# Attention's reciprocals of the sums, from columns to rows: by TensorE and 512-byte rows in place of 4-byte elements

## The chip, the core and the metric

One core of a Trainium2 chip runs the whole program: TensorE (PE, with its weight loads as PEld), VectorE (DVE), ScalarE (ACT), GpSimd (POOL), and SyncE (SP), which issues nearly all transfers from one queue. The metric is the time of one launch on the device in microseconds. Shown are the median of the runs and one profiled execution with its trace.

## The reference

Attention over 32 heads with pooled queries, then two feed-forward stages, which the change leaves alone. The attention, cut to what is computed:

```
q_pool = q.reshape(B, H, S // 2, 2, D).mean(axis=3)          # B 4, H 8, S 1152, D 64
scores = 1 / sqrt(D) * matmul(q_pool, k.transpose(0, 1, 3, 2))
attn = exp(scores - max(scores))
attn = attn / (sum(attn, axis=-1) + 1e-9)
out = matmul(attn, v)
```

## The kernel before

The 32 heads are worked off as 16 pairs (p), each pair in 9 tiles (t) of 128 queries, 144 tiles (g) in all. A tile's 1152 keys stand as 1024 columns, `ps_s` (L82, L85), and a rest of 128 columns, `ps_r` (L95, L98), on 128 partitions; the rest uses 128 of the 512 columns of its PSUM bank, of which there is one. VectorE takes the maximum (L105 over `ps_s`, L106 over `ps_r`), ScalarE the exponentials (L117, L119), whose accumulators give the sums as a column, one number for each query's partition. TensorE transposes the exponentials (L131), VectorE and ScalarE copy them back (L149, L147) into `aw_et`, and TensorE multiplies them by v (L190, "av" below). The result has the queries along its columns, so the reciprocal of the sums is wanted as a row, repeated on 64 partitions for each of the two heads: `aw_rb`.

The way from column to row goes through DRAM, twice in a pair: chunk c = 0 after the fourth tile (t = 3), and c = 1 after the ninth (t = 8). `sums` adds and inverts (L158, L159) and issues the column writes into `rdram`, one element of 4 bytes for each query (two transfers at L164, and for c = 1 two more at L167). `spread` issues the loads that repeat a row of 1024 bytes on 64 partitions (L175, and L177 for the fifth tile, 256 bytes). `out` multiplies av's result by it (L198, L200), which frees the one PSUM bank of av, and issues the store of the pair (L201). av for a chunk is cut into four pieces, one for each of four tiles; the multiply comes in the tile after the last piece.

The order is written out as events with due times (`at`): what is to happen for a tile g stands at g plus a fraction, all events are sorted, and every engine gets its instructions in that order. `sums` is due at g + 2.13, `spread` at g + 5.05, the pieces of av at .5 of each tile, the multiply at 1.11 of the next. The loads of the next pair's q and k (L53, L55; `load_qk`) are due in its first two tiles, v (L60) in the seventh. In between run steps that prepare weights of the next stage: a load `bg_raw` (L295), VectorE steps on `bg_e` (L311 to L330), stores `wi_d` (L338, L339). SyncE issues in program order and waits in its queue for what each transfer needs.

At the end of attention SyncE issues the load of `m_a_wsh` (L387) between the last column writes and the last loads of rows, and the next stage's first matmul (L501) waits until PSUM is free, which is after the last multiply.

Of the kernel before, what the change touches and what calls it, by code (L numbers as in the profile page):

```python
# [5 lines left out]
F32 = mybir.dt.float32  # L6
# [23 lines left out]
def attention(tc, nc, ap, cst, xT, bg, hooks):  # L30
# [5 lines left out]
    with ExitStack() as ctx:  # L36
        wrk = Pool(ctx.enter_context(tc.tile_pool(name="a_wrk", bufs=2, side="right")), "aw")
        early = ctx.enter_context(ExitStack())
        opr = Pool(early.enter_context(tc.tile_pool(name="a_op", bufs=2)), "ao")
        ps = Pool(ctx.enter_context(tc.tile_pool(name="a_ps", bufs=1, space=PSUM)), "ps")  # L40
        ident = cst["ident"]

        KIND = [(0, 0), (1, 0), (0, 1), (1, 1), (0, 2), (1, 2), (0, 3), (1, 3), None]
        NT = NP * NTL
        P = {}
        E, ET, SUM, MX, TP = {}, {}, {}, {}, {}
        rdram = tc.dram_tile([NP, 2, 6, 128], F32, name="rdram")

        def load_qk(p, h):
# [51 lines left out]
        def maximum(g):  # L101

            d = E[g]
            m = d["m"] = wrk([128, 2], F32, "mx", bufs=4)
            nc.vector.tensor_reduce(out=m[:, 0:1], in_=d["s"], op=ALU.min, axis=AX.XY)  # L105
            nc.vector.tensor_scalar(out=wrk([128, 128], F32, "junk", bufs=1), in0=d["r"][:, 0:128], scalar1=m[:, 0:1], scalar2=None,  # L106
                                    op0=ALU.min, op1=ALU.min, accum_out=m[:, 1:2])

# [44 lines left out]
        def sums(p, c):  # L153

            n = 4 if c == 0 else 5
            s = SUM.pop((p, c))
            rs = wrk([128, 6], F32, f"rs{c}")
            nc.vector.scalar_tensor_tensor(out=rs[:, 0:n], in0=s[:, 0:n, 0], scalar=1e-9, in1=s[:, 0:n, 1], op0=ALU.add, op1=ALU.add)  # L158
            nc.vector.reciprocal(out=rs[:, 0:n], in_=rs[:, 0:n])  # L159
            d = rdram[p, c]  # L160
            with nc.allow_non_contiguous_dma(reason="a pair's sums, from columns to rows"):

                for h in range(2):
                    nc.sync.dma_start(d[3 * h:3 * h + 2].rearrange("c q -> q c"), rs[:, h:4:2])  # L164
                if c:
                    for h in range(2):
                        nc.sync.dma_start(d[3 * h + 2:3 * h + 3].rearrange("c q -> q c"), rs[:, 4:5])  # L167
            P[p]["rb", c] = wrk([128, 320], F32, f"rb{c}", bufs=1)

        def spread(p, c):  # L170
            rb, d = P[p]["rb", c], rdram[p, c]
            for h in range(2):
                o = slice(64 * h, 64 * h + 64)
                row = d[3 * h:3 * h + 3].rearrange("c q -> (c q)").unsqueeze(0)
                nc.sync.dma_start(rb[o, 0:256], row[:, 0:256].to_broadcast([64, 256]))  # L175
                if c:
                    nc.sync.dma_start(rb[o, 256:320], row[:, 256 + 64 * h:320 + 64 * h].to_broadcast([64, 64]))  # L177

        AVQ = []

# [40 lines left out]
        def at(time, f, *a):  # L221
            events.append((time, len(events), f, a))
# [6 lines left out]
        for g in range(NT):  # L229
            p, t = divmod(g, NTL)  # L230
            at(g, scores, g)
            at(g + .2, scores_rest, g)
            at(g + .6, maximum, g)
            at(g + 1.15, exps, g)
            at(g + 1.98, transp, g, 0)
            at(g + 2.1, back, g, 0, "v")
            at(g + 2.15, transp, g, 1)
            at(g + 2.4, back, g, 1, "a")
            if t == 3:
                at(g + 2.13, sums, p, 0)  # L240
                at(g + 5.05, spread, p, 0)
                at(g + 3.45, push, p, 0)
            if t == 8:
                at(g + 2.13, sums, p, 1)
                at(g + 5.05, spread, p, 1)
                at(g + 3.45, push, p, 1)
            if p + 1 < NP:
                if t in (0, 1):
                    at(g + .3 if p else g + 1.3, load_qk, p + 1, t)
                if t in (3, 4):  # L250
                    at(g + .3, prep, p + 1, t - 3, nc.gpsimd)
                if t == 6:
                    at(g + .3, load_v, p + 1)
            if t % 9 not in (3, 4, 5) and g > 3:
                at(g + .12, step, "v")
                at(g + .42, step, "a")
# [922 lines left out]
def fused(tc, q, k, v, w_in, w_sp, b_sp, w_out, w_g, w1, w2, consts, out):  # L1179
# [7 lines left out]
    with ExitStack() as ctx, tc.manual_schedule():  # L1187
# [6 lines left out]
        hooks = {"raw": lambda: m1.begin_v(keep([128, 4096], F32R, "wv").rearrange("p (n k c) -> p n k c", n=2, k=4)),  # L1194
                 "S": m1.begin, "x1": m1.begin_x1, "T": lambda: m1.split_x(0, m1.x0), "end": m1.begin_u}
        attention(tc, nc, ap, cst, xT, bg, hooks)
        bgp.close()
        tab = Pool(ctx.enter_context(tc.tile_pool(name="tab", bufs=1, side="right")), "tab")
# [77 lines left out]
```

## Time and profile before

| | us |
|---|---|
| runs of the kernel before | 1138.47, 1144.91 (median), 1147.83 |
| the profiled execution | 1142.15 |
| its span, first to last instruction | 1140.4 |
| TensorE busy in the span | 1017.6 |
| VectorE busy | 743.2 |

Sizes by the page's list of transfers: the two halves of a pair's q have 576 KB each, of its k 320 KB each, so a half of q and k together 896 KB (917 thousand bytes); the first load, of the identity, 64 KB; `m_a_wsh` 1024 and 128 KB. 30,858 of the program's 68,128 packets are under 512 bytes.

How to read it: the busy share is an average over stages with different limits. Attention takes the first 592 us of the span, and a page or an answer for all of it mixes tiles in which the engines follow each other without a gap with tiles in which all of them wait. What ended a wait is what counts. In the rows, "[4.70 <-DMA aw_rb<-rdram]" means that the engine sat idle for 4.70 us and that this transfer's landing ended it; SPq is SyncE's queue; a transfer's piece in the chain of waits runs from its issue to its landing.

### The profile page before, as it was taken

The numbers are of one execution on the slowest core, as the hardware profiler recorded it, in microseconds if no ns is written. First come the engines' busy times: TensorE is split into PE (matmuls) and PEld (weight loads), VectorE is DVE, ScalarE is ACT, GpSimd is POOL, SyncE is SP. The second block draws the span as 40 slices with busy tenths as digits, with TensorE's granted clock in tenths as the row PEclk, the third lists the DMA queues.
The fourth block names the chain that finished last, engine by engine and source line by source line (L and its number), as shares of the span: only waits on it lengthen the run. The fifth ranks groups of instructions, "written<-read, shape, count | busy, mean of one in ns | idle before, by whom it ended". The sixth has DMA issues, their size and how long they took to land.

```text
span 1140.4 us, 19804 instructions
## 1 busy us (share of the span) xinstructions
PE 1017.6 (89%) x7500; PEld 685.5 (60%) x7500; DVE 743.2 (65%) x1329; ACT 595.6 (52%) x1172; POOL 229.1 (20%) x189
## 2 busy tenths in 40 slices
PE   6679878799989969989947999999999999999997
PEld 3234434344444434444436898899777777777775
DVE  5558766577876757766718861423378877888784
ACT  4346645466656646655614332212237767776773
POOL 1001110111110111110025341122121413133221
PEclk9789988999999989989978899999999999999999
DMA  5346745456756756737153211200283314111750
GB/s 153 85 84 103 113 90 124 70 114 113 109 117 126 88 95 121 94 105 144 36 151 111 66 53 39 75 1 1 91 285 143 120 47 176 37 38 50 279 222 26
DMA packets 68128, 116.78 MB, mean 102 GB/s; under 512 B 30858, under 2 KB 39218, under 8 KB 66488
## 3 DMA queue, kind: packets, MB, share of 16 engines
q1 hardware_dynamic: 64304, 104.38, 39.4%
q0 software_dynamic: 3680, 11.02, 2.9%
q8 instruction: 63, 1.03, 0.5%
q14 instruction: 41, 0.34, 0.2%
q10 hardware_dynamic: 40, 0.01, 0.0%
HBM read 165.61 MB, written 19.48 MB: 162 GB/s over the span
## 4 chain that ended last, share of the span: by engine, by line
PE 44%; issue 20%; DMA 19%; DVE 10%; POOL 3%; ACT 2%; SPq 2%; another core or an unknown queue 0%; POOLq 0%; DVEq 0%; ACTq 0%
PE ps_av L190 10%; PE ps_t L131 8%; DMA aw_rb<-rdram 7%; DMA rdram<-aw_rs 6%; PE ps_s L82 5%; DMA er_x<-x,tab_gi 4%; PE m_ps_v L608 4%; PE m_ps_u L556 4%; PE m_ps_u L542 3%; PE m_ps_v L501 3%; POOL er_x L983 2%; PE ps_r L95 2%; DVE aw_et L149 2%; DVE aw_mx L105 2%; PE ps_s L85 1%
## 5 line engine op out<-in xcount | busy, mean ns | idle before, releaser
L131 PEld LDWEIGHTS ps_t<-keep_ident,aw_e 64*128 64x128 f32 x2592 | 107.6, 143 | 225.8 <-DVE aw_et L149 145.0
L190 PE MATMUL ps_av<-aw_et,aw_v 128*64 128x320 f32 (+1 forms) x1152 | 175.3, 433 | 38.2 <-DVE aw_xo L200 38.2
L105 DVE TENSOR_REDUCE aw_mx<-ps_s 128x1 f32<-128x1024 f32 x144 | 174.8, 1214 | 15.4 <-PE ps_s L82 8.4
L131 PE MATMUL ps_t<-keep_ident,aw_e 64*128 64x64 f32 x2592 | 146.3, 239 | 42.8 <-DVE aw_et L149 32.7
L149 DVE COPY aw_et<-ps_t 128x640 f32<-128x640 f32 x144 | 118.7, 824 | 95.4 <-PE ps_t L131 84.3
L119 ACT ACTIVATE aw_e<-ps_s,aw_mx 128x1024 f32<-128x1024 f32 x144 | 159.2, 1105 | 0.0
L82 PE MATMUL ps_s<-ao_k,ao_q 64*128 64x512 f32 x512 | 148.2, 659 | 7.3 <-DMA ao_k<-in_k 5.9
L117 ACT ACTIVATE aw_e<-ps_r,aw_mx 128x128 f32<-128x128 f32 x144 | 52.9, 368 | 163.8 <-DVE aw_junk L106 163.2
L190 PEld LDWEIGHTS ps_av<-aw_et,aw_v 128*64 128x64 f32 x1152 | 74.3, 142 | 89.8 <-DVE aw_xo L200 39.5
L147 ACT ACTIVATE aw_et<-ps_t 128x512 f32<-128x512 f32 x144 | 86.0, 597 | 77.2 <-PE ps_t L131 70.5
L354 DVE TENSOR_TENSOR eb_w2l<-er_r,eb_w2h 128x1024 fp32r<-128x1024 f32 x88 | 103.5, 1218 | 4.6 <-ACT eb_w2h L350 4.4
L354 DVE TENSOR_TENSOR eb_w1l<-er_r,eb_w1h 128x1024 fp32r<-128x1024 f32 x66 | 78.8, 1221 | 34.1 <-ACT eb_w1h L350 34.1
L350 ACT ACTIVATE eb_w2h<-er_r 128x1024 fp32r<-128x1024 f32 x88 | 88.7, 1068 | 0.6 <-PE ep_yp L1056 0.3
L71 POOL TENSOR_TENSOR ao_qr<-ao_qr 128x576 f32<-128x576 f32 x30 | 42.4, 1414 | 213.5 <-DMA ao_qr<-in_q 181.2
L350 ACT ACTIVATE eb_w1h<-er_r 128x1024 fp32r<-128x1024 f32 x66 | 67.8, 1072 | 18.1 <-DMA er_r<-in_w 8.5
L1056 PE MATMUL ep_yp<-eb_w2h,ew_hth 128*128 128x512 f32 x176 | 71.1, 404 | 0.3 <-ACT ew_hth L350 0.3
L1056 PE MATMUL ep_yp<-eb_w2h,ew_htl 128*128 128x512 f32 x176 | 70.2, 399 | 0.2 <-DVE ew_htl L354 0.2
L1056 PE MATMUL ep_yp<-eb_w2l,ew_hth 128*128 128x512 f32 x176 | 69.1, 393 | 0.0
L1062 POOL DMA_INDIRECT out<-ew_y,tab_si x22 | 22.4, 1017 | 202.6 <-DVE ew_y L1061 176.7
L106 DVE TENSOR_SCALAR_CACHE_REDUCE aw_junk<-ps_r,aw_mx 128x128 f32<-128x128 f32 x144 | 50.6, 351 | 19.1 <-PE ps_r L95 0.6
L501 PE MATMUL m_ps_v<-keep_wv,m_a_xh 128*128 128x512 f32 x144 | 47.0, 400 | 14.7 <-issue 13.7
L354 POOL TENSOR_TENSOR bg_l<-bg_e,bg_h 128x256 fp32r<-128x256 f32 x16 | 11.6, 727 | 237.7 <-ACT bg_h L350 237.7
(234 smaller groups left out, 1905.0 us busy)
## 6 DMA issues: line engine op xcount, KB each, us to landing
er_r<-in_w SPq DMA_DIRECT2D x45, 2048.0 KB
ao_qr<-in_q SPq DMA_DIRECT2D x32, 576.0 KB
ao_k<-in_k SPq DMA_DIRECT2D x32, 320.0 KB
aw_v<-in_v SPq DMA_DIRECT2D x16, 576.0 KB
xT<-aw_xo SPq DMA_DIRECT2D x16, 288.0 KB
bg_raw<-in_w_in SPq DMA_DIRECT2D x16, 256.0 KB
aw_rb<-rdram SPq DMA_DIRECT2D x64, 64.0 KB
er_r<-in_w SPq DMA_DIRECT2D x16, 256.0 KB
```

Of the source, the lines that this page charges most:

```text
L82: nc.tensor.matmul(d["s"][:, i, :], r["q", h][rows, 128 * n:128 * n + 128], r["k", h][rows, 0:512], start=True, stop=True)
L105: nc.vector.tensor_reduce(out=m[:, 0:1], in_=d["s"], op=ALU.min, axis=AX.XY)
L117: nc.scalar.activation(out=e[:, 8, :], in_=d["r"][:, 0:128], func=AF.Exp, bias=d["m"][:, 1:2], scale=-1.0, accum_out=s[:, col, 1:2])
L119: nc.scalar.activation(out=e[:, 0:8, :].rearrange("p k c -> p (k c)"), in_=d["s"].rearrange("p i c -> p (i c)"), func=AF.Exp, bias=d["m"][ ...
L131: nc.tensor.transpose(t[:, i, 64 * (k - k0):64 * (k - k0) + 64], E[g]["e"][o, k, :], ident[o, o])
L147: nc.scalar.activation(out=o, in_=i, func=AF.Copy)
L149: nc.vector.tensor_copy(o, i)
L190: nc.tensor.matmul(box["t"][64 * h:64 * h + 64, 0:n], v[:, h, k, :], et[:, k, h, 0:n], start=k == 0, stop=k == 8)
L350: nc.scalar.activation(out=hi, in_=src, func=AF.Copy)
L354: (nc.gpsimd if eng_lo == "p" else nc.vector).tensor_tensor(out=lo, in0=src, in1=hi.bitcast(F32), op=ALU.subtract)
L501: nc.tensor.matmul(pv, xx[xi][:, k, tile(i, j)], wv[:, wj, k, :], start=n == 0, stop=n == 11)
L1056: nc.tensor.matmul(pt, hT[hi][:, c, 128 * o:128 * o + 128], W2[wi][:, f, :], start=f == 0 and (hi, wi) == (0, 0), stop=f == 7 and (hi, wi) ...
```

## The change

The reciprocals stay as they are (L158 and L159 before, L164 and L165 now), but no transfer starts there. `sums_turn`, due at g + 2.25, has TensorE transpose the 4 or 5 columns of reciprocals into as many rows, in columns 128 to 255 of the bank that holds the rest of the scores of tile g + 2 (L171). `maximum` for that tile copies the rows to SBUF (L109), between its two instructions, and SyncE writes them to DRAM as rows of 512 bytes (L110). The last chunk of all has no tile behind it, and does the same in a bank of its own (`sums_last`). `spread` is due one tile earlier, at g + 4.05, and its loads read two rows of 512 bytes where they read one of 1024, since the rows of DRAM now stand in the order of the tiles.

```diff
--- before.py
+++ after.py
@@ -43,7 +43,7 @@
         KIND = [(0, 0), (1, 0), (0, 1), (1, 1), (0, 2), (1, 2), (0, 3), (1, 3), None]
         NT = NP * NTL
         P = {}
-        E, ET, SUM, MX, TP = {}, {}, {}, {}, {}
+        E, ET, SUM, RS, TP = {}, {}, {}, {}, {}
         rdram = tc.dram_tile([NP, 2, 6, 128], F32, name="rdram")
 
         def load_qk(p, h):
@@ -103,6 +103,12 @@
             d = E[g]
             m = d["m"] = wrk([128, 2], F32, "mx", bufs=4)
             nc.vector.tensor_reduce(out=m[:, 0:1], in_=d["s"], op=ALU.min, axis=AX.XY)
+            if "row" in d:
+                q, c, n = d["row"]
+                row = wrk([6, 128], F32, f"row{c}")
+                nc.vector.tensor_copy(row[0:n], d["r"][0:n, 128:256])
+                nc.sync.dma_start(rdram[q, c, 0:n], row[0:n])
+                P[q]["rb", c] = wrk([128, 320], F32, f"rb{c}", bufs=1)
             nc.vector.tensor_scalar(out=wrk([128, 128], F32, "junk", bufs=1), in0=d["r"][:, 0:128], scalar1=m[:, 0:1], scalar2=None,
                                     op0=ALU.min, op1=ALU.min, accum_out=m[:, 1:2])
 
@@ -157,24 +163,31 @@
             rs = wrk([128, 6], F32, f"rs{c}")
             nc.vector.scalar_tensor_tensor(out=rs[:, 0:n], in0=s[:, 0:n, 0], scalar=1e-9, in1=s[:, 0:n, 1], op0=ALU.add, op1=ALU.add)
             nc.vector.reciprocal(out=rs[:, 0:n], in_=rs[:, 0:n])
-            d = rdram[p, c]
-            with nc.allow_non_contiguous_dma(reason="a pair's sums, from columns to rows"):
-
-                for h in range(2):
-                    nc.sync.dma_start(d[3 * h:3 * h + 2].rearrange("c q -> q c"), rs[:, h:4:2])
-                if c:
-                    for h in range(2):
-                        nc.sync.dma_start(d[3 * h + 2:3 * h + 3].rearrange("c q -> q c"), rs[:, 4:5])
+            RS[p, c] = rs
+
+        def sums_turn(p, c, g):
+
+            n = 4 if c == 0 else 5
+            nc.tensor.transpose(E[g]["r"][0:n, 128:256], RS.pop((p, c))[:, 0:n], ident)
+            E[g]["row"] = (p, c, n)
+
+        def sums_last(p, c):
+
+            t = ps([128, 512], F32, "r")
+            nc.tensor.transpose(t[0:5, 0:128], RS.pop((p, c))[:, 0:5], ident)
+            row = wrk([6, 128], F32, f"row{c}")
+            nc.vector.tensor_copy(row[0:5], t[0:5, 0:128])
+            nc.sync.dma_start(rdram[p, c, 0:5], row[0:5])
             P[p]["rb", c] = wrk([128, 320], F32, f"rb{c}", bufs=1)
 
         def spread(p, c):
+
             rb, d = P[p]["rb", c], rdram[p, c]
             for h in range(2):
                 o = slice(64 * h, 64 * h + 64)
-                row = d[3 * h:3 * h + 3].rearrange("c q -> (c q)").unsqueeze(0)
-                nc.sync.dma_start(rb[o, 0:256], row[:, 0:256].to_broadcast([64, 256]))
+                nc.sync.dma_start(rb[o, 0:256].rearrange("p (c q) -> p c q", c=2), d[h:4:2].unsqueeze(0).to_broadcast([64, 2, 128]))
                 if c:
-                    nc.sync.dma_start(rb[o, 256:320], row[:, 256 + 64 * h:320 + 64 * h].to_broadcast([64, 64]))
+                    nc.sync.dma_start(rb[o, 256:320], d[4:5, 64 * h:64 * h + 64].to_broadcast([64, 64]))
 
         AVQ = []
 
@@ -238,11 +251,16 @@
             at(g + 2.4, back, g, 1, "a")
             if t == 3:
                 at(g + 2.13, sums, p, 0)
-                at(g + 5.05, spread, p, 0)
+                at(g + 2.25, sums_turn, p, 0, g + 2)
+                at(g + 4.05, spread, p, 0)
                 at(g + 3.45, push, p, 0)
             if t == 8:
                 at(g + 2.13, sums, p, 1)
-                at(g + 5.05, spread, p, 1)
+                if g + 2 < NT:
+                    at(g + 2.25, sums_turn, p, 1, g + 2)
+                else:
+                    at(g + 2.25, sums_last, p, 1)
+                at(g + 4.05, spread, p, 1)
                 at(g + 3.45, push, p, 1)
             if p + 1 < NP:
                 if t in (0, 1):
```

Where it moves instructions. TensorE, after the fourth tile of the second pair; `ps_s` and `ps_r` are the scores and their rest, `ps_t` transposes, `ps_av` av, `aw_rs` the reciprocals. Before:

```order
L82 MATMUL ps_s_655<-ao_k_10_156,ao_q_12_229 128x512 x2
L131 MATMUL ps_t_665<-keep_ident_65,aw_e_627 128x64 x8
L95 MATMUL ps_r_678<-ao_k_10_156,ao_q_12_229 128x128
L190 MATMUL ps_av_549<-aw_et_292,aw_v_88 64x320 x6
L131 MATMUL ps_t_691<-keep_ident_65,aw_e_675 128x64 x10
```

Now:

```order
L82 MATMUL ps_s_657<-ao_k_10_156,ao_q_12_229 128x512 x2
L137 MATMUL ps_t_664<-keep_ident_65,aw_e_629 128x64 x8
L95 MATMUL ps_r_677<-ao_k_10_156,ao_q_12_229 128x128
L171 MATMUL ps_r_677<-keep_ident_65,aw_rs_57_661 4x128
L203 MATMUL ps_av_551<-aw_et_294,aw_v_88 64x320 x6
```

One transpose into the same bank as the rest has come in, between the rest and av. After a ninth tile it stands between the rest and the next ten transposes instead.

VectorE, after the ninth tile of the first pair (`aw_mx` the maximum, `aw_row` the new rows). Before:

```order
L158 SCALAR_TENSOR_TENSOR aw_rs_39_476<-aw_sum_20_267 128x5
L159 RECIPROCAL aw_rs_39_476<-aw_rs_39_476 128x5
L105 TENSOR_REDUCE aw_mx_510<-ps_s_467 128x1
L106 TENSOR_SCALAR aw_junk_512,aw_mx_510<-ps_r_497,aw_mx_510 128x128
L149 COPY aw_et_528<-ps_t_514 128x5x128
```

Now:

```order
L164 SCALAR_TENSOR_TENSOR aw_rs_40_478<-aw_sum_19_264 128x5
L165 RECIPROCAL aw_rs_40_478<-aw_rs_40_478 128x5
L105 TENSOR_REDUCE aw_mx_508<-ps_s_469 128x1
L109 COPY aw_row_44_510<-ps_r_494 5x128
L112 TENSOR_SCALAR aw_junk_514,aw_mx_508<-ps_r_494,aw_mx_508 128x128
L155 COPY aw_et_530<-ps_t_516 128x5x128
```

The copy of the rows has come in between the two instructions of the maximum.

SyncE's queue at the same place, from the second half of the next pair's q and k to the load of the rows. Before:

```order
L164 DMA rdram<-aw_rs_39_476 128x2x1 x2
L167 DMA rdram<-aw_rs_39_476 128x1 x2
L53 DMA ao_qr_15_499<-in_q 128x1152
L55 DMA ao_k_16_501<-in_k 128x640
L338 DMA wi_d<-bg_h_504 128x256
L339 DMA wi_d<-bg_l_505 128x256
L175 DMA aw_rb_40_483<-rdram 64x256
L177 DMA aw_rb_40_483<-rdram 64x64
```

Now:

```order
L53 DMA ao_qr_15_497<-in_q 128x1152
L55 DMA ao_k_16_499<-in_k 128x640
L356 DMA wi_d<-bg_h_502 128x256
L357 DMA wi_d<-bg_l_503 128x256
L110 DMA rdram<-aw_row_44_510 5x128
L188 DMA aw_rb_45_513<-rdram 64x2x128
L190 DMA aw_rb_45_513<-rdram 64x64
```

Four column writes ahead of q and k have gone, and one write of five rows has come in behind them.

## Rows read from the trace of the kernel before

**Rows 1.** The page, part 4: the chain that ended last, by line.
```profile
PE ps_av L190 10%; PE ps_t L131 8%; DMA aw_rb<-rdram 7%; DMA rdram<-aw_rs 6%; PE ps_s L82 5%; DMA er_x<-x,tab_gi 4%; PE m_ps_v L608 4%; PE m_ps_u L556 4%; PE m_ps_u L542 3%; PE m_ps_v L501 3%; POOL er_x L983 2%; PE ps_r L95 2%; DVE aw_et L149 2%; DVE aw_mx L105 2%; PE ps_s L85 1%
```

**Rows 2.** Waits of 0 to 590 us: waiter <- releaser: total us, times, longest.
```profile
PE ps_av L190 <- DVE aw_xo L200: 38.2, 7, 8.2
...
DVE bg_e L311 <- DMA bg_raw<-in_w_in: 10.7, 1, 10.7
```

**Rows 3.** The chain of waits, 165 to 200 us: start, us, what.
```profile
165.31 0.38 SPq L164
...
166.25 8.49 DMA rdram<-aw_rs
...
175.31 10.80 DMA aw_rb<-rdram
...
186.81 1.98 PE ps_av L190 x8
...
189.51 1.81 PE ps_s L82 x4
...
195.87 1.01 PE ps_av L190 x8
...
197.34 0.92 PE ps_s L82 x4
```

**Rows 4.** Stretches: us, busy by engine, then clock, DMA share, GB/s.
```profile
2.00:9.00 7.00, 2.47 (x6) 1.20 (x6) 1.99 (x5) 0.02 (x1) 0.00 (x0) 1.00 0.97 346
167.00:177.00 10.00, 9.42 (x96) 4.92 (x96) 7.45 (x14) 7.06 (x18) 0.00 (x0) 1.00 0.75 31
```

**Rows 5.** Stretches from one L200 to the next, columns as in rows 4.
```profile
78.88:111.31 32.43, 30.52 (x290) 15.40 (x292) 25.15 (x50) 19.18 (x46) 4.95 (x5) 0.93 0.58 111
...
258.41:290.05 31.64, 29.16 (x300) 14.84 (x299) 24.89 (x51) 19.66 (x47) 4.94 (x5) 1.00 0.66 113
290.05:320.37 30.32, 29.16 (x302) 14.90 (x301) 23.96 (x51) 19.79 (x47) 4.88 (x5) 1.00 0.79 118
355.39:388.00 32.61, 29.21 (x300) 14.82 (x299) 23.84 (x50) 19.98 (x48) 5.57 (x6) 1.00 0.69 126
529.23:560.33 31.10, 30.00 (x290) 15.29 (x292) 22.46 (x44) 18.55 (x44) 0.00 (x0) 0.95 0.42 107
```

**Rows 6.** Timeline, 0 to 9 us: start, us, engine, line, operation, [idle <- releaser].
```profile
1.21 0.42 SPq L53 DMA_DIRECT2D ao_qr<-in_q  x1
...
5.04 0.29 DVE L71 TENSOR_TENSOR ao_qr<-ao_qr 128x128 f32<-128x128 f32 x1 [5.04 <-DMA ao_qr<-in_q]
```

**Rows 7.** Timeline, 570 to 593 us: the end of attention.
```profile
573.33 5.07 PE L190 MATMUL ps_av<-aw_et,aw_v 128*64 128x320 f32 x36
...
573.53 0.88 SPq L164 DMA_DIRECT2D rdram<-aw_rs  x2
...
591.29 0.42 DVE L198 TENSOR_TENSOR aw_xo<-ps_av,aw_rb 128x256 f32<-128x256 f32 x1 [13.95 <-DMA aw_rb<-rdram]
```

**Rows 8.** Groups by line, whole span: count | busy us, mean ns | idle before.
```profile
L1041 PE MATMUL ep_ht<-keep_ident,ew_h 128*128 128x128 f32 x176 | 23.0, 273 | 0.7 <-DVE ew_h L1030 0.7
L106 DVE TENSOR_SCALAR_CACHE_REDUCE aw_junk<-ps_r,aw_mx 128x128 f32<-128x128 f32 x144 | 50.6, 351 | 19.1 <-PE ps_r L95 0.6 <-DVE aw_mx L105 0.5
L200 DVE TENSOR_TENSOR aw_xo<-ps_av,aw_rb 128x64 f32<-128x64 f32 x16 | 3.5, 216 | 7.7 <-DMA aw_rb<-rdram 7.7
```

**Rows 9.** Timeline of VectorE, 177 to 187 us: behind a fourth tile.
```profile
180.68 0.82 DVE L149 COPY aw_et<-ps_t 128x640 f32<-128x640 f32 x1 [1.18 <-PE ps_t L131]
186.20 0.42 DVE L198 TENSOR_TENSOR aw_xo<-ps_av,aw_rb 128x256 f32<-128x256 f32 x1 [4.70 <-DMA aw_rb<-rdram]
```

**Rows 10.** Timeline, 164 to 168 us: behind a ninth tile.
```profile
165.09 0.19 DVE L159 RECIPROCAL aw_rs<-aw_rs 128x5 f32<-128x5 f32 x1
...
165.66 0.52 PE L131 MATMUL ps_t<-keep_ident,aw_e 64*128 64x64 f32 x10 [0.42 <-ACT aw_et L147]
...
167.65 0.46 PE L131 MATMUL ps_t<-keep_ident,aw_e 64*128 64x64 f32 x8 [0.56 <-DVE aw_et L149]
```

## The prediction

> **What bounds the kernel now.** I read the page's chain of work first. Below TensorE's shares it has two transfers that belong to nothing but the reciprocals: the load `aw_rb<-rdram` with 7% and the write `rdram<-aw_rs` with 6% of the span [rows 1]. That is 13% of 1140 us, some 148 us, for transfers of a few kilobytes. Not all of it can be won, since the chain follows a long transfer even where engines worked beside it, so I went to the waits of the attention stage. There TensorE stood still 38.2 us in 7 waits for VectorE's multiply L200, and VectorE stood 10.7 us in one wait for `bg_raw`, a load of weights that has nothing to do with the sums [rows 2]. That second wait is the clue to the rest.
>
> The chain over one of the 32 hand-overs shows the order [rows 3]: the column writes are issued from 165.31 and the last of them lands 8.49 us after 166.25; the load of the rows into `rb`, issued at 175.31, takes another 10.80 us; at 186.20 the multiply may run. The transfer rates say why [rows 4]. At the start of the kernel the queue moves 346 GB/s. In the ten microseconds behind the column writes it moves 31 GB/s, with the engines marked 0.75 busy. The 4-byte elements make the queue crawl for all that stands behind them: the next q and k, the rows, `bg_raw`.
>
> A stall also costs clock. Right after it eight av matmuls take 1.98 us and four of the scores 1.81, at half clock; 9 us later they take 1.01 and 0.92 [rows 3]. So the whole price of a stall is best read from the length of a pair, cut at L200. The 14 pairs from 78.88 to 560.33 take 481.45 us, 34.4 each; the three at full clock took 31.64, 30.32 and 32.61, on average 31.52 [rows 5]. The granted clock in these rows (0.93 in the first, 1.00 in the three) is a mean of the two levels, 1.2 and 2.4 GHz; the first begins right behind a stall.
>
> **The change, part by part.** *The column writes go.* Per pair 2 and 4 transfers of 4-byte elements, 1,280 elements, become two of 4 and 5 rows of 512 bytes. If the crawl goes with them, all 14 pairs run like the three clean ones: 481.45 - 14 x 31.52 = 40 us. The ends of this are 57 us (all like 30.32) and 25 us (all like 32.61).
>
> *The first pair* (up to 78.88) has two stalls: VectorE's 10.7 us for `bg_raw`, and 8.2 us, the longest wait of TensorE for L200 [rows 2]; one half-clock stretch after them falls in this pair, 0.97 + 0.89 = 1.9 us by the pieces above. `bg_raw` must still be loaded. A load on an idle queue lands 3.8 us after its issue (1.21 to 5.04 [rows 6]) behind about 650 KB, which at 346 GB/s is 1.9 us, so some 1.9 us are fixed, an estimate. I keep 2.5 us of the wait: 10.7 + 8.2 + 1.9 - 2.5 = 18 us; ends 15 and 19.
>
> *The tail.* The last column writes are issued from 573.53 on, and VectorE idles 13.95 us until 591.29, waiting for the last load of rows; the av matmuls end at 573.33 + 5.07 = 578.4 [rows 7]. After the change the row is issued about 0.8 us later than the first of these, at 574.3 (turn, copy and their hand-overs), lands 1.9 us later, the rows' load is issued by 578.3 behind 1.2 MB of `m_a_wsh` (3.4 us at 346 GB/s, done by then) and lands near 580.5. Gain 591.3 - 580.5 = 10.8, of which I take 10; ends 4 and 12 (nothing goes below 578.4 plus a turn).
>
> The landing of a write of 4 or 5 rows stands in no row. It lies between the load's 1.9 us and the column write's 8.49; I take 1.9 because few packets are nearer to the first. With 8.49 the tail would gain 4 us and the hand-overs below would use up their whole slack. The Trainium skill, "DMA: Bandwidth & Descriptors" (Anatomy of one DMA), puts a fixed 2.0 us on a transfer, most of it the receipt of the last byte, heaviest to HBM; with it the sum stays the same, and no row shows it for a write this small.
>
> *The turns are added*: 32 transposes on TensorE, 32 copies on VectorE. Nearest rows: a 128x128 transpose 273 ns; VectorE from PSUM 216 ns at 64 columns and 351 ns for L106 at 128 [rows 8]. I take 0.27 for the turn and 0.21 for the copy. After the fourth tile the turn stands between the scores' rest and av, where TensorE has no idle time; VectorE there idles 1.18 us before its next copy [rows 9], which covers the copy. So 16 x 0.27 = 4.3 us count. After the ninth tile TensorE idles 0.42 us just where the turn goes in, but 2 us later it waits 0.56 us for a copy of VectorE's that stands behind the new one [rows 10]: there the copy counts, 16 x 0.21 = 3.4 us. Together 7 us (one turn is the tail's). Were everything serial, with L106's duration for the copy, it would be 32 x 0.62 = 20 us; the lower end is 0. The Trainium skill, "TensorE: Matmul & The Clock Gate" (Part 4: PE-mode transpose), has 390 ns for a transpose in isolation and about 275 in a kernel; this case's 273 agrees with the second, and with the first the sum would be 2 us longer.
>
> *New waits.* TensorE's turn waits for the reciprocal; behind it in TensorE's order stand av or the next transposes. The reciprocal ends at 165.28, and TensorE falls idle at 165.66 - 0.42 = 165.24 [rows 10], so the turn waits under 0.2 us. VectorE's copy waits for the turn, with the 1.2 us maximum ahead of it as cover. SyncE's row write now stands behind the second half of the next q and k (917 KB). Between the sums (165.31) and the moment at which VectorE asked for `rb` (186.20 - 4.70 = 181.5) lie 16.2 us [rows 3, 9]. Needed: copy done near 166.7, 917 KB at 346 GB/s 2.7 us, 1.9 to land, four issues 2 us, 1.9 to land: about 175. Six microseconds are spare. SyncE's load of the rows moves one tile ahead, and waits there only for the row's landing; what stands behind it isn't due for two tiles.
>
> **Sum.** 40 + 18 + 10 - 7 = 61 us off the profiled execution's 1142.15 (span 1140.4 and 1.75 around it): **1081 us**. The median of the three runs is 1144.91, 2.8 above; within the range.
>
> **Rivals.** *Part of the stalls stays*, because the row stands behind 917 KB and the chain eats its slack in some pairs. It begins where the queue needs over 6 us more than the 2.7 for them, that is under 917/8.7 = 105 GB/s. The crawl's 31 GB/s would do it, the 346 would not. With half of the pairs' and first pair's gain lost (29 us): 1110.
>
> *The writes weren't the cause*: the queue is slow in itself and `rb` comes as late as now. For it: q and k move in the slow stretch too. Against: 346 GB/s on the same shapes at the start. Then only the turns' 7 us are new: 1149.
>
> *Slower.* If any small write to DRAM takes 8.49 us to land and slows what follows, the row, now behind q and k, comes later than today: q and k 10 us, as long as the slow stretch of [rows 4] (at its 31 GB/s they would take 30), the row 8.5 to land, its load 10.8, 29 us against 16.2, 13 late in each of 15 hand-overs, 195 us, less the stalls of now (40 + 18) and plus 7: 1142 + 144 = 1286. It decides once the chain is over 16.2 + 58/15 = 20 us. The row's size speaks against it: 5 packets instead of 768. The Trainium skill, "DMA: Bandwidth & Descriptors" (Specifications), has transfers below 512 bytes do a read-modify-write; by it the new rows escape and the old elements don't, and no row of the trace shows a 512-byte write.
>
> **How the numbers follow.** The forecast has a chance of 0.82, the partial stalls 0.10, no effect 0.04, slower 0.04. The range must leave out at most 2 in 10: below, the pairs at 30.32 (17 us more) and a cheaper turn give 1142 - 57 - 18 - 10 + 4 = 1061, taken as 1062; above, the pairs at 32.61, the tail's 4 and the serial turns' 20 give 1142 - 25 - 18 - 4 + 20 = 1115, all at once; I take 1106, which holds most of it and part of the partial stalls. One per cent, 11 us, is about what a measurement of this kernel tells from no change: faster 0.92 (forecast and partial), same 0.04, slower 0.04.
>
> **What would show it.** In the changed profile: no wait of VectorE's multiply for `aw_rb` over 1 us; TensorE's 38.2 us gone; no stretch of 31 GB/s; pairs of 30 to 32.5 us at a clock near 1.00; 32 transposes of about 0.27 us with under 0.2 us of wait; the last multiply at about 530, where it was at 591. Wrong would be: `rdram<-aw_row` landing after more than 5 us, waits on `aw_rb` left in the second hand-over of a pair, or pairs over 33 us with no stall in them, which would put the loss on the turns.

## The result and the profile after

| | before | after |
|---|---|---|
| median of 4 runs, us | 1141.69 (1136.23 to 1147.83) | 1063.6 (1060.92 to 1071.63) |
| ratio to before, with its 95% interval | | 0.9326 (0.9253 to 0.94) |
| the profiled execution, us | 1142.15 | 1063.56 |
| its span | 1140.4 | 1061.7 |
| mean granted clock of TensorE | 0.954 | 0.983 |
| packets | 68,128 | 50,495 |

The change makes the kernel 78 us faster. The forecast was 1081, with a range of 1062 to 1106. The result is near the lower end: the direction was right, and the gain was 17 us larger than the sum. Times below are medians of all runs; a ratio and its interval take only the runs in the faster of the two states that the program shows, so a ratio need not be the quotient of two medians.

The page of after, part 4, the chain that ended last, by engine and by line (it answers to [rows 1]):

```profile
PE 75%; DVE 10%; DMA 7%; issue 4%; ACT 2%; POOL 1%; SPq 0%; POOLq 0%; DVEq 0%; ACTq 0%
PE ps_av L203 15%; PE ps_t L137 11%; PE ep_yp L1074 8%; PE ps_s L82 8%; PE ep_hp L1041 6%; DMA er_x<-x,tab_gi 4%; PE m_ps_v L626 4%; PE m_ps_u L574 4%; PE m_ps_u L560 3%; PE m_ps_v L519 3%; PE ep_hp L1034 3%; PE ps_r L95 3%; DVE aw_mx L105 2%; PE ps_s L85 2%; DMA ao_qr<-in_q 1%
```

Both transfers of the reciprocals, 7% and 6% of the chain before, are gone from these lines, and TensorE has 75%, where it had 44%.

Waits of 0 to 590 us in after (waiter <- releaser: total us, times, longest), which answer to [rows 2]:

```profile
PE ps_t L137 <- DVE aw_et L155: 12.0, 17, 2.2
PE ps_r L171 <- DVE aw_rs L165: 6.0, 10, 1.4
...
DVE aw_xo L211 <- DMA aw_rb<-rdram: 4.6, 1, 4.6
DVE bg_e L329 <- DMA bg_raw<-in_w_in: 2.7, 1, 2.7
...
SPq L188 <- DMA rdram<-aw_row: 30.4, 13, 4.5
```

TensorE no longer waits for the multiply; that row, 38.2 us before, is missing. The wait for `bg_raw` fell from 10.7 to 2.7 us. Of the multiply's waits for the rows only the tail's is left. SyncE still waits for the row to land, up to 4.5 us, and nobody waits for SyncE. New are TensorE's waits for the reciprocal at the turn (`ps_r` L171).

Stretches of after: us, busy by engine, granted clock, DMA share, GB/s. Four go from one L213 (the multiply of before's L200) to the next; the last one holds the loads of q and k just ahead of a ninth tile's sums:

```profile
60.57:90.88 30.31, 29.55 (x302) 14.98 (x302) 24.07 (x52) 19.78 (x47) 5.11 (x5) 1.00 0.36 118
90.88:124.03 33.15, 31.03 (x302) 15.67 (x302) 25.70 (x53) 19.79 (x47) 4.93 (x5) 0.95 0.34 109
...
245.90:278.34 32.44, 30.96 (x302) 15.59 (x302) 25.69 (x52) 19.78 (x47) 5.06 (x5) 0.95 0.34 111
278.34:309.85 31.51, 29.49 (x302) 14.99 (x302) 25.33 (x53) 19.80 (x47) 5.04 (x5) 1.00 0.36 114
```
```profile
254.60:259.60 5.00, 4.91 (x50) 2.48 (x46) 4.01 (x9) 3.75 (x9) 0.53 (x1) 1.00 0.91 289
```

Eleven of the 14 pairs from 60.57 to 491.63 take 30.1 to 30.7 us. The three long ones are those of 33.15, 32.44 and 31.51. The slow stretch is gone: where q and k move with a DMA share of 0.91, they move at 289 GB/s, and not at 31 with a share of 0.75 as in [rows 4].

Where the time went, by the cuts at L200 and L213: the first pair ends 18.3 us earlier (78.88 to 60.57), the 14 pairs take 50.4 less (481.45 to 431.06), the tail to the last such multiply 9.4 less (31.30 to 21.91), and the rest of the program 0.6 less. Together 78.7, the difference of the spans.

### The profile page after: what moved, and what is told of

Read it like the earlier page. It is cut to its first block, busy times and chain, and to the rows that moved or that the text cites. A ratio compares the mean times of both kernels' runs of the same rounds, so it can differ in the third digit from the quotient of the medians.

```text
span 1061.7 us, 19763 instructions
## 1 busy us (share of the span) xinstructions
PE 1008.2 (95%) x7532; PEld 679.5 (64%) x7532; DVE 748.7 (71%) x1361; ACT 595.3 (56%) x1172; POOL 225.5 (21%) x189
## 2 busy tenths in 40 slices
DMA packets 50495, 116.75 MB, mean 110 GB/s; under 512 B 8986, under 2 KB 21586, under 8 KB 48856
## 3 DMA queue, kind: packets, MB, share of 16 engines
q1 hardware_dynamic: 46672, 104.37, 29.0%
q0 software_dynamic: 3680, 11.02, 3.2%
## 4 chain that ended last, share of the span: by engine, by line
PE 75%; DVE 10%; DMA 7%; issue 4%; ACT 2%; POOL 1%; SPq 0%; POOLq 0%; DVEq 0%; ACTq 0%
PE ps_av L203 15%; PE ps_t L137 11%; PE ep_yp L1074 8%; PE ps_s L82 8%; PE ep_hp L1041 6%; DMA er_x<-x,tab_gi 4%; PE m_ps_v L626 4%; PE m_ps_u L574 4%; PE m_ps_u L560 3%; PE m_ps_v L519 3%; PE ep_hp L1034 3%; PE ps_r L95 3%; DVE aw_mx L105 2%; PE ps_s L85 2%; DMA ao_qr<-in_q 1%
## 5 line engine op out<-in xcount | busy, mean ns | idle before, releaser
L137 PEld LDWEIGHTS ps_t<-keep_ident,aw_e 64*128 64x128 f32 x2592 | 104.0, 140 | 193.1 <-DVE aw_et L155 130.3
L203 PE MATMUL ps_av<-aw_et,aw_v 128*64 128x320 f32 (+1 forms) x1152 | 168.9, 420 | 0.0
L137 PE MATMUL ps_t<-keep_ident,aw_e 64*128 64x64 f32 x2592 | 143.5, 235 | 15.8 <-DVE aw_et L155 12.0
L82 PE MATMUL ps_s<-ao_k,ao_q 64*128 64x512 f32 x512 | 141.7, 632 | 7.2 <-DMA ao_k<-in_k 6.0
L372 DVE TENSOR_TENSOR eb_w2l<-er_r,eb_w2h 128x1024 fp32r<-128x1024 f32 x88 | 103.5, 1217 | 4.2 <-ACT eb_w2h L368 4.1
L203 PEld LDWEIGHTS ps_av<-aw_et,aw_v 128*64 128x64 f32 x1152 | 72.0, 137 | 49.0 <-issue 4.1
L372 DVE TENSOR_TENSOR eb_w1l<-er_r,eb_w1h 128x1024 fp32r<-128x1024 f32 x66 | 78.7, 1221 | 33.6 <-ACT eb_w1h L368 33.6
L71 POOL TENSOR_TENSOR ao_qr<-ao_qr 128x576 f32<-128x576 f32 x30 | 43.2, 1442 | 72.6 <-DMA ao_qr<-in_q 72.1
L95 PE MATMUL ps_r<-ao_k,ao_q 64*128 64x128 f32 x256 | 57.2, 304 | 0.0
```

Source lines behind the costliest of these rows:

```text
L82: nc.tensor.matmul(d["s"][:, i, :], r["q", h][rows, 128 * n:128 * n + 128], r["k", h][rows, 0:512], start=True, stop=True)
L95: nc.tensor.matmul(d["r"][:, 0:128], r["q", h][rows, 128 * n:128 * n + 128], r["k", h][rows, 512:640], start=True, stop=True)
L137: nc.tensor.transpose(t[:, i, 64 * (k - k0):64 * (k - k0) + 64], E[g]["e"][o, k, :], ident[o, o])
L203: nc.tensor.matmul(box["t"][64 * h:64 * h + 64, 0:n], v[:, h, k, :], et[:, k, h, 0:n], start=k == 0, stop=k == 8)
L372: (nc.gpsimd if eng_lo == "p" else nc.vector).tensor_tensor(out=lo, in0=src, in1=hi.bitcast(F32), op=ALU.subtract)
```

## The experiments

Three theories were told apart. **Crawl**: the column writes of 4-byte elements hold up whatever else the queue moves. **Order**: the way from sums to rows is shorter, since the load of the rows is issued a tile earlier; the writes are harmless. **Count**: it is the number of packets that costs, whatever their size. The kernel before took 1154.19, 1155.19, 1165.25, 1164.66 and 1156.45 us (the third and fourth are single runs) beside the five sets of runs below, and 1141.69 beside the changed kernel. So a ratio is to the kernel before of its own set, and a few us between kernels of different sets are not read as an effect. The changed kernel's own four runs lie 11 us apart.

**The column writes alone, added to the changed kernel.**

```diff
         rdram = tc.dram_tile([NP, 2, 6, 128], F32, name="rdram")
+        xdram = tc.dram_tile([NP, 2, 6, 128], F32, name="xdram")
...
             RS[p, c] = rs
+            x = xdram[p, c]
+            with nc.allow_non_contiguous_dma(reason="columns"):
+                for h in range(2):
+                    nc.sync.dma_start(x[3 * h:3 * h + 2].rearrange("c q -> q c"), rs[:, h:4:2])
+                if c:
+                    for h in range(2):
+                        nc.sync.dma_start(x[3 * h + 2:3 * h + 3].rearrange("c q -> q c"), rs[:, 4:5])
```

> The changed kernel, with the old column writes issued again at their old place, 4 bytes per element, into a scratch tensor that nobody reads; the rows of the changed kernel still carry the result, so the shorter chain is kept. Theory 1 (the 4-byte writes themselves slow the queue for all that stands behind them): most of the 78 us comes back, 1110 to 1150 us, with a stretch near 31 GB/s behind the column writes, bg_raw's wait near 10 us again and TensorE waiting for the multiply again. Theory 2 (the gain is the shorter chain, the earlier load of the rows, not the writes): 1062 to 1075 us, no slow stretch.

Measured: 1156.27 us (10 runs), 1.0073 times the kernel before (1.0015 to 1.0131), where the changed kernel has 0.9326. All of the gain is gone, by writes that nobody reads. Waits of 0 to 590 us, then a stretch right behind a ninth tile's column writes (columns as above):

```profile
SPq L196 <- DMA rdram<-aw_row: 144.6, 23, 12.5
...
PE ps_av L211 <- DVE aw_xo L221: 26.1, 12, 5.0
...
DVE bg_e L337 <- DMA bg_raw<-in_w_in: 11.7, 1, 11.7
```
```profile
163.00:171.00 8.00, 7.88 (x80) 4.12 (x80) 6.70 (x10) 5.35 (x13) 1.29 (x2) 1.00 0.93 33
```

TensorE waits for the multiply again, `bg_raw` comes 11.7 us late, and the queue moves 33 GB/s with its engines marked 0.93 busy. Crawl predicted this, and the chain from sums to rows is the short one here, so the shorter chain does not protect. It came out 6 us above the range given for crawl; that range was set beside 1141.69 for the kernel before, which took 1154.19 in this set. Whether it costs something to have the old writes and the new rows together is not shown.

**The order alone, both ways.** In the kernel before the load of the rows moves a tile ahead; in the changed kernel it moves back.

```diff
-                at(g + 5.05, spread, p, 0)
+                at(g + 4.05, spread, p, 0)
...
-                at(g + 5.05, spread, p, 1)
+                at(g + 4.05, spread, p, 1)
```

> The kernel before with only the load of the rows moved one tile ahead, to g + 4.05; the column writes stay. Theory 2 (the earlier load takes the stalls away): most of the gain, 1070 to 1100 us. Theory 1 (the queue crawls behind the 4-byte writes, and the load with it): 1130 to 1150, as before, since the load stands in the same crawl; it gains at most the time from 181.5 back to its issue, a few us.

> The changed kernel with the load of the rows due at g + 5.05 again, as before the change: only the move of that load is undone. Theory 1 (the column writes made the queue slow; the earlier load is slack that nobody needs): 1062 to 1070 us, and the rows still land before the multiply. Theory 2 (the earlier load is what took the stalls away): 1090 us or more, with TensorE's waits for the multiply back.

Measured, one run of each: 1164.88 for the kernel before with the early load (1155.19 without, 1141.32 to 1162.7), and 1061.71 for the changed kernel with the late one. Where the column writes stand, the early load saves nothing; TensorE's waits for the multiply are still there:

```profile
PE ps_av L190 <- DVE aw_xo L200: 50.3, 10, 8.8
...
DVE aw_xo L198 <- DMA aw_rb<-rdram: 43.6, 9, 7.4
```

The move of `spread` is worth nothing that can be told in either direction, and order falls.

**How many, how small, how close.** The added writes were then changed in one thing at a time: to rows of 512 bytes, as many of them (a scrap tile as source); to 4-byte elements with a gap between one and the next; and to GpSimd's queue (`nc.gpsimd.dma_start` in place of `nc.sync.dma_start`, elements side by side). The edit for 512 bytes, against the run with the column writes; for 64, 16 and 8 bytes the last dimension of `xdram` is 16, 4 and 2:

```diff
-        xdram = tc.dram_tile([NP, 2, 6, 128], F32, name="xdram")
+        xdram = tc.dram_tile([NP, 2, 6, 128, 128], F32, name="xdram")
...
-                    nc.sync.dma_start(x[3 * h:3 * h + 2].rearrange("c q -> q c"), rs[:, h:4:2])
+                    nc.sync.dma_start(x[3 * h:3 * h + 2, :, 0].rearrange("c q -> q c"), rs[:, h:4:2])
...
-                        nc.sync.dma_start(x[3 * h + 2:3 * h + 3].rearrange("c q -> q c"), rs[:, 4:5])
+                        nc.sync.dma_start(x[3 * h + 2:3 * h + 3, :, 0].rearrange("c q -> q c"), rs[:, 4:5])
```

> As the run with the column writes added, with the same number of packets, 1,280 in a pair, but each is a row of 512 bytes (contents without meaning, nobody reads them), so 655 KB a pair in place of 5 KB. Theory 3 (the number of packets is what slows the queue): as slow as the run with the 4-byte elements, 1110 to 1150 us. Theory 1 (their size of 4 bytes): 655 KB at 346 GB/s is 1.9 us of transfer a pair beside other work, 1062 to 1080 us, no stretch below 100 GB/s behind them.

> As the run with the column writes added, but each 4-byte element goes into a 512-byte row of its own; the count of elements and transfers is the same, 1,280 in a pair, and nobody reads them. If it is the smallness of each write that slows the queue: like the run with the column writes in one place, 1110 to 1150 us. If it is that 128 elements fall on the same few hundred bytes of DRAM and wait for each other: 1062 to 1080 us, packets near their 178 ns median.

> As the run with each element in a 512-byte row of its own (1064.6 us), but with 64 bytes from element to element, so that eight of them share 512 bytes, where in the column writes of the kernel before 128 share them. If all that matters is that elements share 512 bytes: like the column writes side by side, 1120 to 1160 us. If the cost grows with how many share them (8 in place of 128): in between, 1066 to 1100. If what collides is a piece of 64 bytes or less: 1060 to 1070, like the 512-byte spacing.

> As the run with 64 bytes from element to element (1067.5 us), with 16 bytes instead: four elements in 64 bytes, 32 in 512. If elements have to share 64 bytes to collide, and the price goes with how many are written into one such piece one after the other (16 in the column writes of the kernel before, four here): a part of the loss, 1075 to 1130 us. If any sharing gives the whole loss: 1130 to 1165. If they have to touch each other: 1060 to 1070.

> As the runs with 64 and 16 bytes from element to element (1067.5 and 1068.0 us), with 8 bytes: eight elements in 64 bytes, none touches its neighbour. If the price goes with how many elements fall into one piece of 64 bytes one after the other (1 and 4 in the two runs cost about 3 us, 16 in the column writes nearly all): at eight a part of the loss, 1080 to 1130 us. If elements must touch: 1062 to 1070 again. If the step to the whole loss lies between 16 and 8 bytes: 1130 to 1165.

> As the run with the column writes added (1156 us), but GpSimd issues them from its own queue, while q, k, the rows and bg_raw stay on SyncE's. If the writes block only the transfers of their own queue behind them: 1062 to 1080 us, with q's packets near their median of 178 ns. If they hold up something that the queues share (the 16 engines or the memory): 1120 to 1165, and q's packets on SyncE's queue again at a mean of 500 ns and more.

Measured (single runs, but for the first row with 4 and the row of 4 bytes with 10), each with four readings of its trace: SyncE's waits for the row to land, VectorE's first wait for `bg_raw`, the mean time of the 6,144 packets of 4,608 bytes (q's and v's), and the start of attention's last multiply:

| added to the changed kernel, per pair | us | SyncE's wait, us | `bg_raw`, us | packet of q or v, ns | last multiply at, us |
|---|---|---|---|---|---|
| nothing | 1063.6 | 30.4 | 2.7 | 221 | 513.54 |
| 1,280 rows of 512 bytes | 1063.18 | 43.9 | 3.0 | 239 | 511.71 |
| 1,280 elements, 512 bytes apart | 1064.6 | 47.9 | 3.3 | 243 | 514.04 |
| 64 bytes apart | 1067.51 | 48.4 | 2.9 | 249 | 516.51 |
| 16 bytes apart | 1067.99 | 64.5 | 3.6 | 274 | 517.29 |
| 8 bytes apart | 1074.55 | 73.0 | 6.2 | 296 | 523.73 |
| 4 bytes apart (side by side) | 1156.27 | 144.6 | 11.7 | 648 | 606.26 |
| the same on GpSimd's queue | 1149.56 | 176.4 | 12.4 | 341 | 589.39 |

The extreme rows of the table in the profile, waits of 0 to 590 us of the run with 8 bytes and of the run with 512:

```profile
DVE aw_xo L219 <- DMA aw_rb<-rdram: 9.3, 2, 8.0
DVE bg_e L337 <- DMA bg_raw<-in_w_in: 6.2, 1, 6.2
...
PE ps_av L211 <- DVE aw_xo L221: 1.1, 1, 1.1
```
```profile
SPq L196 <- DMA rdram<-aw_row: 47.9, 15, 4.4
```

Count falls: 655 KB more in as many packets cost nothing that can be told. That the elements are small is not it either: 28,061 packets of 4 bytes in the program, the same number as with the writes side by side, cost nothing that can be told (1064.6) when each has 512 bytes to itself. Nor is it that SyncE waits for the sums ahead of q and k: the spaced writes have the same source at the same place in the queue. The price is in how close the elements fall. From 512 bytes to 8 it grows in SyncE's wait, in the packets and in the end of attention (`bg_raw` dips at 64), and reaches the time with force only in the last step. At 16 bytes and more the time is within the changed kernel's own runs; the one run with 8 bytes is 11 us longer, between the ranges that its expectation gave, and its trace shows 10 of them by the end of attention; at 4 bytes it is 93, or some 85 by the two ratios.

The chain from sums to multiply has slack, and until it is used up a slower queue costs little; the waits show this, 1.1 us for the multiply at 8 bytes, 26.1 at 4. But the queue itself also steps there, 296 to 648 ns, so slack is not all of it. Whether elements must touch for the full price or only lie in a small enough piece of memory is not told apart: as the gap shrinks, so does the whole span of addresses. What in the path to memory is slow, no row names.

The run on GpSimd's queue shows that the price isn't bound to SyncE's queue. Its rows and `bg_raw`, with no column write among them, are held up as much, and the multiply's longest wait is longer than on one queue:

```profile
DVE aw_xo L219 <- DMA aw_rb<-rdram: 41.3, 4, 14.6
...
PE ps_av L211 <- DVE aw_xo L221: 30.6, 4, 14.4
```

Its expectation named 500 ns for q's packets; those of q and v took 341, so part of them did escape, but the rows and `bg_raw` did not. By the end of attention the writes cost 76 us here and 93 on SyncE's queue. They are not the same packets: on SyncE's queue they add 22,016 to the page's count (68,688 against 46,672), on GpSimd's 3,072 (6,752 against 3,680), with the elements in packets of 64 and 32 bytes. So the price doesn't need 1,280 packets a pair; how such a packet writes its elements, no row shows. The Trainium skill, "DMA: Bandwidth & Descriptors" (Issuing engines are not separate DMA queues), says that transfers run on the same 16 DMA engines whichever engine issues them; that the loads of SyncE's queue are slowed by writes of GpSimd's (1149.56 us against 1156.27) agrees. The rule that the prediction cited from the same page, that transfers under 512 bytes do a read-modify-write, gives no price by itself: the elements 512 bytes apart are as small as the others and cost next to nothing.

**The price of the turns.** The turn and its copy are left out, and the rows are written from a scrap tile, so the multiplication is not by the reciprocals; attention's transfers stay. `J[0]` is the scrap tile of the maximum, with four buffers in place of one.

```diff
-                nc.vector.tensor_copy(row[0:n], d["r"][0:n, 128:256])
-                nc.sync.dma_start(rdram[q, c, 0:n], row[0:n])
...
+            if "row" in d:
+                nc.sync.dma_start(rdram[q, c, 0:n], J[0][0:n])
...
-            nc.tensor.transpose(E[g]["r"][0:n, 128:256], RS.pop((p, c))[:, 0:n], ident)
```

> The changed kernel without the turn on TensorE and without the copy on VectorE in 31 of the 32 chunks: the rows that go to DRAM are taken from the scrap tile of the maximum, so the multiplication is by numbers that are not the reciprocals; the transfers are as in the changed kernel. The difference to the changed kernel is the price of the turns. By the prediction 7 us: 1056 to 1057 us. If the turns cost what TensorE's waits for the reciprocal in the changed trace add up to (6.0 us in 10 waits) and 31 x 0.27 us besides: 14 us, 1049. If they lie in idle time: under 2 us, 1062 or more.

Measured: 1062.77 us, 1060.28 to 1066.51, 0.9258 times the kernel before of its set (0.9174 to 0.9343), where the changed kernel has 0.9326 (0.9253 to 0.94): the turns can't be told from nothing by the time. The time is also not quite of the same work. The stages behind attention get other numbers here, and by the page the queue moves 4.2 MB more (108.56 MB against 104.37); they took 550.79 us for 548.16. In the trace a pair without them is shorter by about 0.16 us (the medians of 14 pairs are 30.26 and 30.42). The second pair of this kernel, to set beside the 30.31 of after:

```profile
59.85:90.00 30.15, 29.09 (x300) 14.84 (x300) 23.90 (x51) 19.76 (x47) 5.00 (x5) 1.00 0.36 119
```

Over 15 or 16 pairs that is 2 to 3 us, less than half of the 7 that were counted. Attention's last multiply comes 5.8 us earlier (507.71 for 513.54); what is over the 2 to 3 us lies in single long pairs, 33.15, 32.44 and 31.51 with the turns and 31.73 and 31.04 without.

**The long pairs.** In after three of the 32 additions at L164 take 1.36 us, where the others take 0.15 to 0.16. The timeline of after, 103.5 to 106.5 us, shows the first (start, us, engine, line, operation, [idle <- releaser]):

```profile
104.17 1.45 POOL L71 TENSOR_TENSOR ao_qr<-ao_qr 128x576 f32<-128x576 f32 x1 [4.97 <-DMA ao_qr<-in_q]
...
104.28 1.36 DVE L164 SCALAR_TENSOR_TENSOR aw_rs<-aw_sum 128x5 f32<-128x5 f32 x1
...
105.92 0.27 PE L171 MATMUL ps_r<-keep_ident,aw_rs 128*5 128x128 f32 x1 [1.43 <-DVE aw_rs L165]
```

VectorE's addition of 128x5 starts 0.11 us after GpSimd's addition on q and ends with it; TensorE's turn waits for it. Two edits tried to take this away: the sums earlier in VectorE's order, and the addition as a reduction with one input in place of an operation with two.

```diff
-                at(g + 2.13, sums, p, 0)
+                at(g + 2.105, sums, p, 0)
...
-                at(g + 2.13, sums, p, 1)
+                at(g + 2.105, sums, p, 1)
```

> The changed kernel with the sums due at g + 2.105 in place of g + 2.13, ahead of a copy and of a step on the weights in VectorE's order, so that the reciprocal is ready before TensorE comes to the turn. If the 6.0 us of TensorE's waits for the reciprocal, 1.3 to 1.4 us in the longest, lie on the path: 3 to 6 us below the changed kernel, 1057 to 1061, and the three long pairs (33.15, 32.44, 31.50 us) become like the others at 30.4. If the wait only moves to what VectorE does later for it: within 2 us of the changed kernel, 1062 to 1066.

```diff
-            nc.vector.scalar_tensor_tensor(out=rs[:, 0:n], in0=s[:, 0:n, 0], scalar=1e-9, in1=s[:, 0:n, 1], op0=ALU.add, op1=ALU.add)
+            nc.vector.tensor_reduce(out=rs[:, 0:n], in_=s[:, 0:n, :], op=ALU.add, axis=AX.X)
```

> The changed kernel with the two sums of a query added by a reduction with one input from SBUF, in place of L164's operation with two (the 1e-9 is left out; each sum holds a term of 1). In the changed kernel three of the 31 additions take 1.36 us in place of 0.15 to 0.16, each exactly as long as GpSimd's L71 runs, and TensorE's turn waits 1.3 to 1.4 us for each. If what stretches is the operation with two inputs from SBUF: none over 0.3 us, the three long pairs (33.15, 32.44, 31.50 us) fall to 30.4, 1058 to 1062 us. If the hold on VectorE only moves to the next such operation, or takes the reduction too: 1062 to 1067.

Measured: 1065.82 us (1061.45 to 1071.59) and 1065.01 (1057.65 to 1070.05), by ratio 0.9273 (0.9223 to 0.9324) and 0.926 (0.9197 to 0.9323): neither can be told from the changed kernel. With the sums first, TensorE's waits at the turn are gone, but the three pairs still take 30.81, 33.00 and 31.60 us, another takes 31.83, and the waits for the copies grew from 12.0 to 17.9 and from 2.3 to 4.7 us:

```profile
PE ps_t L137 <- DVE aw_et L155: 17.9, 21, 2.5
...
PE ps_t L137 <- ACT aw_et L153: 4.7, 19, 0.7
```

With the reduction, the timeline of 102 to 107 us and of 406 to 409:

```profile
103.07 1.40 POOL L71 TENSOR_TENSOR ao_qr<-ao_qr 128x576 f32<-128x576 f32 x1 [5.08 <-PE ps_t L137]
103.08 0.16 DVE L164 TENSOR_REDUCE aw_rs<-aw_sum 128x5 f32<-128x10 f32 x1
...
105.32 1.41 POOL L71 TENSOR_TENSOR ao_qr<-ao_qr 128x576 f32<-128x576 f32 x1
...
105.68 1.20 DVE L340 TENSOR_SCALAR bg_m<-bg_m 128x256 int32<-128x256 f32 x1
```
```profile
406.64 1.40 POOL L71 TENSOR_TENSOR ao_qr<-ao_qr 128x576 f32<-128x576 f32 x1 [4.61 <-PE ps_s L82]
406.80 1.53 DVE L336 SCALAR_TENSOR_TENSOR bg_e<-bg_raw,bg_e 128x256 int32<-128x256 int32 x1
```

The reduction isn't held: it runs beside L71 in 0.16 us. But at 406.80 the hold falls on L336, which stands just ahead of the sums and makes the turn wait 1.34 us all the same. The three long pairs fell to 30.56, 30.41 and 30.47 us, one new one takes 32.36, and attention's last multiply comes 4.9 us earlier (508.60 for 513.54); in this execution the rest of the program took 6.9 us more (555.05 for 548.16), with the clock at 0.50 from 757.6 to 774.7, where after has 1.00. In this run the reduction meets L71 only once, in the first of the three pairs. So the rows show the hold on the addition behind the long pairs, and once that a reduction escapes it; a gain in the time is not shown, for the hold moves to other operations.

## Why the prediction was right, and where it was off

**The cause.** Right: the column writes made the queue crawl, and put back alone they take all of the gain away. The reason given was too wide. Elements of 4 bytes do no such harm by their size (1064.6 us with 512 bytes to each), and not only what stands behind them on their queue is slowed (1149.56 us from GpSimd's). The change takes away all of these writes, so the forecast did not depend on it. The rival *the writes weren't the cause* (1149) is out by the run that adds them back. *Part of the stalls stays* and *slower* needed a row that lands late behind 917 KB. The order of the code has it there, but in the run SyncE no longer waits for the sums ahead of q and k: the two halves of the pair around 104 us are issued by 101.5, the row at 107.18, and the next issue on the queue, which needs it landed, is at 108.38. The row landed within 1.2 us there. The 2.0 us that the prediction cites from the Trainium skill, "DMA: Bandwidth & Descriptors" (Anatomy of one DMA), stand in a section on transfers that GpSimd issues; for this write of SyncE's the 1.2 us decide. Where q and k are issued just ahead it takes longer than the assumed 1.9: the row issued at 230.58, behind a load of k issued at 228.25, holds the next issue until 235.07. The slack of 6 us took that in.

**The first pair**: 18 counted, 18.3 measured. The wait for `bg_raw` that I kept, 2.5 us, is 2.7. **The tail**: 10 counted, 9.4 measured; the rows come 4.56 us after VectorE was ready for them. That is a wait over the 1 us that the prediction named as a sign, but its own sum for the tail left 3 to 4.

**The 14 pairs**: here the sum was mis-sized; the result stayed inside the range because its lower end took all pairs at 30.32. It had 40 us less for the crawl and some 6 more for the turns, 34 net; measured are 50.4. The term that failed is "all 14 pairs run like the three clean ones", 31.52 us each [rows 5]. Full clock was taken as the mark of a clean pair, and two of the three weren't clean. The pair of 31.64 us contains an operation that GpSimd stretched (timeline of before, 275 us):

```profile
275.19 1.41 POOL L71 TENSOR_TENSOR ao_qr<-ao_qr 128x576 f32<-128x576 f32 x1 [4.31 <-DMA ao_qr<-in_q]
275.23 1.65 DVE L318 SCALAR_TENSOR_TENSOR bg_e<-bg_raw,bg_e 128x256 int32<-128x256 int32 x1
```

In most other places that operation takes 0.41, so 1.2 us of the pair are this. The pair of 32.61 has VectorE idle 2.2 us at 362.31; what held it I didn't settle. Only in the one of 30.32 did I find no such hold or idle time, and the lower end that I had worked out from it, 57 us, is the better estimate: 11 of the 14 pairs after take 30.1 to 30.7.

**The turns**: 7 counted, 2 to 3 measured by the pair's usual length. The transposes take the 0.27 us that were taken, and the copy 0.27 where 0.21 was taken. What failed is where they count. After the ninth tile neither shows in the pair's length, and after the fourth only about 0.16 to 0.2 of the 0.27 does. The waits of the turn were put under 0.2 us; most are, but in the three long pairs they are 1.3 to 1.4, which costs 5 to 6 us in all (33.15, 32.44 and 31.51 against 30.42). The prediction didn't have that: in the rows it used, VectorE's addition was never beside GpSimd's. That both together come near the 7 is luck.

Net for the 14 pairs: 17.6 us from the pair's length (14 x (31.52 - 30.26)) and 4 from the turns, less some 5 for the long pairs, is the 16 that were missing.

## What to carry to other kernels

When a transfer's rate is far below what the same shape reaches elsewhere in the trace while its engines are marked busy, look at what was issued just ahead of it; here 5 KB a pair of 4-byte writes side by side cost 85 to 93 us in all. Turn a column into a row on an engine before it goes to DRAM, or at least leave a gap between its elements (with 16 bytes from one to the next no loss could be told here); GpSimd's queue did not help. And before a mean over "clean" stretches goes into a sum, look through each for its longest wait and its stretched operations: the shortest stretch may be the only clean one.

## What the runs showed of the hardware that was not expected

- 1,280 writes of 4 bytes a pair leave the time as it is when 512 bytes lie from one element to the next (1064.6 us against 1063.6), cost about 11 us at 8 bytes, and 93 (85 by the ratios) side by side (single runs, but for the last and the changed kernel).
- Their cost falls on transfers of another queue too (1149.56 us with the writes on GpSimd's queue, where they are recorded as fewer and larger packets).
- An operation of VectorE with two inputs from SBUF, started while GpSimd's L71 runs, is held until L71 ends: 1.36 us for 0.15, 1.53 and 1.65 for 0.41. A reduction with one input ran beside it in 0.16, the one time that the two met. The Trainium skill, "SBUF — State Buffer" (SBUF: two separate sides), describes this: a pair of ports that VectorE and GpSimd share, held by one of them for a whole instruction, and used by VectorE when it has two inputs in SBUF. The rows above agree, the free reduction included. Two inputs are not the whole condition: L340, with one, took 1.20 us beside L71 and 0.28 in most other places. The same section of the Trainium skill adds VectorE's two-port modes; which mode L340 ran in, no row shows.
